# The closing product of batches 3 to 6 split into a second level of seven products, in two parts, with its three adds on GpSimd

## Chip, core and metric

The kernel runs on one core of a Trainium2 chip. The metric is the device time of one execution in microseconds; the median of repeated runs is compared. Engines are named as in the profile: PE is the matrix engine (PEld its weight loads), DVE is VectorE, ACT is ScalarE, POOL is GpSimd, SP issues DMAs.

## What is computed

Inputs are `x` (8 batches, 8 heads, 512 tokens, 64 wide), `state` (8 batches, 8 heads, 32 rows, 64 wide), `w_in` (512 x 2048) and `w_out` (2048 x 512). Cut to what matters:

```python
a  = softmax(x @ state.T / 8);  xread = a  @ state     # 512 rows per batch
a2 = softmax(state @ x.T / 8);  sread = a2 @ x         # 32 rows per batch
rows = concat([xread, sread])                          # 544 rows per batch, 512 wide over the heads
out = gelu(rows @ w_in) @ w_out                        # 4352 x 512
```

## The kernel before

**Batches and slots.** The kernel works through the eight batches. For the batch it is at, `b`, the token rows go through `mm1` (line 506: per block `m` of 128 of the 2048 hidden columns, two matmuls of 512 columns, followed on ACT by the gelu of line 513 into the tile `g`). In the loop over batches 2 to 7 the sixteen blocks are done in eight slots `p`, two blocks each (`M(k, k + 1)`); each slot also does pieces of other work: the second matrix product of the batch before, and the attention of the batch after. The order on each engine is written out by hand: the program order is the queue order of that engine (`manual_schedule`), and semaphores are put where one engine needs another's data or buffer.

**The second product.** `g @ w_out` is not done plainly in batches 1 to 7. The 512 tokens, the 2048 hidden columns and the 512 outputs are each halved, and the eight block products are replaced by seven (named 1 to 7), at the price of sums and differences of blocks. `chain` names the left operand of each; for 5, 6, 7 and 3 it is a sum that DVE makes (`g_sum`, line 637), for 1, 2 and 4 it is a block of `g`. The right operands are blocks of `w_out` or the differences `ws` made once by `w_diff`. One product is `x_mm` (line 647): two blocks of 128 tokens times eight blocks of hidden columns, so 16 matmuls of 256 columns each, with 16 weight loads. The results are combined: `snap` copies a PSUM bank to SBUF on ACT (line 670), `add` on DVE (line 666) makes pieces of the output `oh`.

**Order of the products.** For batch `b`, product 2 is made in slots 5 and 6 and product 4, which this text calls the closing unit, in slot 7 of the batch's own loop (`X(b, "4")`). Products 1, 6, 5 and 7 follow in slots 0 to 3 of the next loop and product 3 in slot 5. The result of product 4 lies in the tile `c4` and is read only in slot 3 of the next loop, by `c21` after product 7. In slot 0 of the next loop the order on PE is: two blocks of `mm1`, then product 1.

**Product 2 is already split once more.** `sub_sums` makes four small sums on DVE (line 721, 128x512 bf16 each). `sub_a` makes four products of four matmuls each, 128 columns wide (line 727), in the four quarters of one PSUM bank, and ACT copies the bank into the tile `qa` (line 741). `sub_b` adds products 6 and 3 to two of the same quarters and overwrites a third with product 7; it therefore has to wait for that copy. ACT copies the bank again into `qb` (line 749), and three DVE adds (line 666, `c<-qb`, `c<-c,qa`, `c<-qa`) put the result `c2` together. Between `sub_a` and `sub_b` stand the two `mm1` blocks of slot 6. `w_subs` (line 595) made the four differences of the weights, `q_w`, early in the kernel.

**Buffers.** The pool `cpool` has one buffer per tag. Before, `qa` uses the tag `s5` and `qb` the tag `u`, which the copies of products 5 and 6 use too. The four PSUM buffers `f` go round among `mm1`, the scores and half of `p_all`; the other four banks (`o0` to `o3`) belong to the products, and slot 5 borrows them for `p_all` (line 441, the product of states and `w_in` for the next batch), whose results ACT and DVE cast into `P` (lines 1002 and 1307). In `p_all` the group `f = 3` writes the bank that product 3 has just used, so it waits for the DVE add `oh<-xp,u` of product 3.

**GpSimd.** In slot 0 POOL waits for a gelu (`hold_for`, line 1016), issues the load of a later batch (`load_x`, line 117) and rearranges the batch after next (`rearr`, line 225), whose transpose SP issues in slot 3 (line 278). In slot 5 it makes the second rearrangement (`rearr_ones`, line 235).

**Last batch.** In the loop of batch 7 `read_out_slot` interleaves the seven products of the 256 state rows (`SR`, line 866) with the products of batch 6.

Of the kernel before, what the change touches and what calls it, by code (L numbers as in the profile page):

```python
# [17 lines left out]
def kernel(  # L18
# [8 lines left out]
    nc = tc.nc  # L27
# [551 lines left out]
        return {"1": b11, "2": b21, "3": b22}.get(name) if name in "123" else w_t[name]  # L579

    QN = NH // 2
    q_w = persist.tile([128, 4, MH // 2, QN], BF16, name="q_w", tag="mix3")

    def w_sub(k, n):
        return b21[:, MH // 2 * k:MH // 2 * k + MH // 2, QN * n:QN * n + QN]

    def w_subs(which):
        for i in which:
            x, y = (
                (w_sub(1, 1), w_sub(1, 0)),  # L590
                (w_sub(0, 1), q_w[:, 0]),
                (w_sub(0, 1), w_sub(1, 1)),
                (w_sub(0, 0), q_w[:, 1]),
            )[i]
            nc.vector.tensor_tensor(out=q_w[:, i], in0=x, in1=y, op=ALU.subtract)

    def sub_rhs(name):
        if name in "123":
            return {"1": w_sub(1, 0), "2": w_sub(0, 0), "3": w_sub(0, 1)}[name]
        return q_w[:, "5674".index(name)]  # L600

    xs = {}
    left, right = slice(0, NH), slice(NH, d_model)
# [68 lines left out]
    def X(b, name):  # L672
        bank = BANK[name]
        first = name in "2154"
        if first:
            xs[b, bank] = otile([128, 2, NH], "xp", bank)
        ps = xs[b, bank]
        x_mm(ps, x_lhs(b, name), w_rhs(name), first)
        if name == "2":
            if b > 1:  # L680
                snap(b, "c2", "c2", ps)
        elif name == "4":
            snap(b, "c4", "c4", ps)
        elif name == "1":
            for h in range(2):
                xs[b, "o", h] = hpool.tile([128, 2, d_model], FP32, name="oh", tag=f"oh{h}")
            add(xs[b, "o", 0][:, :, left], ps, xs[b, "c2"])
            x_out(b, 0, left)
        elif name == "6":
            snap(b, "u", "u", ps)  # L690
        elif name == "5":
            snap(b, "s5", "s5", ps)
# [12 lines left out]
    def c21(b):  # L705
        add(xs[b, "o", 1][:, :, left], xs[b, 1], xs[b, "c4"])

    def sub_q(b):
        def q(h, k):
            g = g_q(b, 0, 0)  # L710
            return g[:, MH // 2 * k:MH // 2 * k + MH // 2, 128 * h:128 * h + 128]

        return q

    def sub_sums(b):
        t = apool.tile([128, 4, MH // 2, 128], BF16, name="gsub", tag="gsum")
        got = xs[b, "sub"] = {}
        for i, name in enumerate("5673"):
            x, y, op = chain(name, sub_q(b), got)
            got[name] = t[:, i]  # L720
            nc.vector.tensor_tensor(out=t[:, i], in0=x, in1=y, op=op)

    def sub_mm(b, name, at, start=False):
        lhs = chain(name, sub_q(b), {})[0] if name in "124" else xs[b, "sub"][name]
        rhs = sub_rhs(name)
        for m in range(MH // 2):
            nc.tensor.matmul(  # L727
                xs[b, 0][:, at, :],
                lhsT=lhs[:, m, :],
                rhs=rhs[:, m, :],  # L730
                start=(start and m == 0),
                stop=(m == MH // 2 - 1),
                skip_group_check=True,
            )

    def sub_a(b):
        xs[b, 0] = otile([128, 4, QN], "xp", 0)
        for at, name in enumerate("2145"):
            sub_mm(b, name, at, at == 0)
        xs[b, "qa"] = cpool.tile([128, 4, QN], FP32, name="qa", tag="s5")  # L740
        nc.scalar.copy(out=xs[b, "qa"], in_=xs[b, 0])

    def sub_b(b):
        sub_mm(b, "6", 1)
        sub_mm(b, "3", 3)
        sub_mm(b, "7", 0, True)
        qa = xs[b, "qa"]
        qb = cpool.tile([128, 4, QN], FP32, name="qb", tag="u")
        nc.scalar.copy(out=qb, in_=xs[b, 0])  # L749
        c = xs[b, "c2"] = c_tile("c2")  # L750
        c = c.rearrange("p j (n w) -> p j n w", n=2)
        add(c[:, 0], qb[:, 1:2, :].broadcast_to([128, 2, QN]), qb[:, 0:4:3, :])
        add(c[:, 1], c[:, 0, 0:1, :].broadcast_to([128, 2, QN]), qa[:, 2:4, :])
        add(c[:, 0, 0, :], qa[:, 1, :], qa[:, 0, :])

    def rows_out(h, js, ns, eng):
        b = B - 1
# [24 lines left out]

    def L5():
        b = B - 1
        xs[b, "s5"] = c_tile("s5")
# [131 lines left out]

    def R(name):
        def c_new(n):
            rs[n] = cpool.tile([128, NH], FP32, name="r_" + n, tag="r_" + n)  # L920
# [19 lines left out]
        snaps = {"2": "c2", "4": "c4", "6": "u", "5": "s5"}  # L940
        if name in snaps:
            nc.scalar.copy(out=c_new(snaps[name]), in_=ps)
        elif name == "1":
            for h in range(2):
                rs["o", h] = opool.tile([128, d_model], FP32, name="osb", tag="osb")
            add(rs["o", 0][:, left], ps, rs["c2"])
        elif name == "7":
            add(rs["o", 1][:, right], ps, rs["s5"])
            add(rs["o", 1][:, left], ps, rs["c4"])
            r_out(1)  # L950
        elif name == "3":
            add(rs["o", 0][:, right], ps, rs["u"])
            r_out(0)
# [73 lines left out]
    def read_out_slot(p):  # L1027
        c, b, k = B - 2, B - 1, 16 * (B - 1) + 2 * p
        if p == 0:
            sr_x("34")  # L1030
            M(k, k + 1)
            g_sum(c, "56")
            SR("3", 0)
            SR("4", 0)
            X(c, "1")
            sr_x("167")
            SR("5", 0)
            SR("2", 0)
            sr_w("7")
        if p == 1:  # L1040
            M(k, k + 1)
            SR_gelu("52", 0)
            X(c, "6")
            SR("1", 0)
            SR("6", 0)
        if p == 2:
            M(k, k + 1)
            SR_gelu("6", 0)
            SR("7", 0)
            SR_gelu("7", 0)  # L1050
            g_sum(c, "7")
            X(c, "5")
            SR("3", 1)
            SR("4", 1)
            g_sum(c, "3")
        if p == 3:
            M(k, k + 1)
            SR("5", 1)
            SR("2", 1)
            SR_gelu("52", 1)  # L1060
            X(c, "7")
            c22(c)
            SR("1", 1)
            c21(c)
            x_out(c, 1)
            SR("6", 1)
        if p == 4:
            M(k, k + 1)
            SR_gelu("6", 1)
            SR("7", 1)  # L1070
            SR_gelu("7", 1)
            X(c, "3")
# [86 lines left out]
    M(8, 9)  # L1159
    M(10, 11)  # L1160
    mm2_m(0, 8)
    w_subs((0, 1))
    atr(1)
    w_subs((2, 3))
    mm2_m(0, 9)
    burst([(1, 1), (0, 3)])
    mm2_m(0, 10)
# [54 lines left out]
    for b in range(2, B):  # L1222
        nb = b + 1
        for p in range(8):
# [24 lines left out]
                w_diff("7")  # L1249
            if p < 5 and nb < B:  # L1250
                if p == 0:
                    g_sum(b - 1, "56")
                if p == 2:
                    if b % 2:
# [23 lines left out]
            if nb == B:  # L1278
                if p == 5:
                    R("2")  # L1280
                    r_sum("73")
                    R("4")
                    sub_sums(b)
                if p == 6:
                    R("1")
                    sub_a(b)
                    R("6")
                    sub_b(b)
                    R("5")
                if p == 7:  # L1290
                    X(b, "4")
# [1 line left out]
            if p == 5:  # L1293
# [11 lines left out]
                sub_a(b)  # L1305
                for _, f, ps in rest:
                    nc.scalar.copy(out=Ps[nb][:, 0, f * 512:(f + 1) * 512], in_=ps[0])
            if p == 6:
                sub_b(b)
# [47 lines left out]
```

## Time and profile before

| what | value |
|---|---|
| median of three runs | 201.92 us (201.89 to 202.7) |
| the profiled execution: its own time | 202.25 us |
| its span in the profile | 200.3 us |
| PE busy | 193.9 us (97%) |
| DVE busy | 155.1 us (77%) |
| ACT busy | 145.6 us (73%) |
| POOL busy | 48.1 us (24%) |
| granted PE clock | 9 tenths or more in every slice; 1.00 in the result |

The profile is of one execution. Its page gives the busy time of each engine, the chain of work that ended last, and groups of instructions with their mean duration. The timeline gives instructions of one engine in order of time, with equal neighbours merged into one row (`x16` is sixteen of them; its second number is from the first start to the last end). Matmuls overlap, so the pace of PE is read from the starts of successive rows, not from the duration of one.

### The profile page before, as it was taken

How to read it: one execution, taken by the hardware profiler on the slowest of the kernel's cores; microseconds unless marked ns; L12 is line 12 of the kernel's file. 1: busy time of each engine (PE TensorE's matmuls, PEld its weight loads, DVE VectorE, ACT ScalarE, POOL GpSimd, SP SyncE). 2: the span in 40 equal slices, each digit the busy share in tenths (PEclk: the TensorE clock that was granted, in tenths of full speed). 3: DMA queues.
4: the chain of work that ended last, by engine and by line, in shares of the span. 5: the costliest groups of instructions: out<-in, count | busy, mean ns of one | idle time of the engine just before them, and what ended most of it. 6: DMA issues, size and time to landing. Idle time of an engine off the chain costs nothing.

```text
span 200.3 us, 5055 instructions
## 1 busy us (share of the span) xinstructions
PE 193.9 (97%) x2102; PEld 134.3 (67%) x2107; DVE 155.1 (77%) x279; ACT 145.6 (73%) x264; POOL 48.1 (24%) x65
## 2 busy tenths in 40 slices
PE   7899999999999999999999999999999999999993
PEld 2533544465767777767777787677776888878893
DVE  2963796969989769975997798849966897984863
ACT  3785577699896799569966997599948778775120
POOL 8972504543403444040504300030000000000000
PEclk9999999999999999999999999999999999999999
DMA  5999999976494959680797025420024010030044
GB/s 192 197 174 202 206 199 201 183 136 142 84 149 77 241 65 164 141 214 0 77 188 209 5 67 95 138 75 27 28 107 106 0 55 0 7 153 0 18 146 157
DMA packets 40567, 23.16 MB, mean 116 GB/s; under 512 B 21856, under 2 KB 39136, under 8 KB 40544
## 3 DMA queue, kind: packets, MB, share of 16 engines
q0 software_dynamic: 13984, 8.10, 29.9%
q1 hardware_dynamic: 25728, 14.22, 27.5%
q10 hardware_dynamic: 832, 0.52, 0.8%
q8 instruction: 16, 0.26, 0.5%
q14 instruction: 7, 0.06, 0.1%
HBM read 17.30 MB, written 8.91 MB: 131 GB/s over the span
## 4 chain that ended last, share of the span: by engine, by line
PE 86%; DMA 5%; POOL 4%; ACT 2%; issue 0%; DVE 0%; POOLq 0%
PE xp L647 36%; PE hp L506 26%; DMA xb<-in_x_dram 5%; PE xp L727 5%; PE op L548 3%; PE sp L866 3%; PE rp L932 3%; POOL w_in_bf L105 2%; PE op L532 2%; PE xp L773 2%; PE pt L333 2%; ACT P L1002 1%; PE p_ps L441 1%; PE sr L962 1%; POOL sbd L95 1%; POOL w_out_bf L113 1%
## 5 line engine op out<-in xcount | busy, mean ns | idle before, releaser
L513 ACT ACTIVATE g<-hp 128x512 bf16<-128x512 f32 x124 | 67.1, 614 | 17.0 <-PE hp L506 16.8
L506 PE MATMUL hp<-AT,P 128*128 128x512 bf16 x248 | 62.2, 379 | 0.0
L647 PEld LDWEIGHTS <-gsum 128*128 128x128 bf16 x416 | 40.4, 98 | 8.9 <-issue 0.4
L647 PE MATMUL xp<-ws,gsum 128*128 128x256 bf16 x320 | 38.2, 273 | 0.0
L506 PEld LDWEIGHTS <-P 128*128 128x128 bf16 x248 | 23.0, 98 | 19.4 <-ACT P L452 0.7
L647 PEld LDWEIGHTS <-g 128*128 128x128 bf16 x240 | 23.3, 98 | 4.8
L637 DVE TENSOR_TENSOR gsum<-g 128x2048 bf16<-128x2048 bf16 x14 | 17.0, 1218 | 0.6 <-ACT g L513 0.6
L225 POOL COPY x<-xb 128x1024 bf16<-128x1024 bf16 x12 | 12.2, 1044 | 18.5 <-DMA xb<-in_x_dram 18.5
L235 POOL COPY xo<-xb 128x1024 bf16<-128x1024 bf16 x12 | 12.2, 1043 | 14.1 <-PE sr L962 13.9
L647 PE MATMUL xp<-w_out_bf,g 128*128 128x256 bf16 x128 | 15.3, 273 | 0.0
L647 PE MATMUL xp<-ws,g 128*128 128x256 bf16 x112 | 13.4, 273 | 0.0
L1016 POOL COPY hold<-g 128x1 bf16<-128x1 bf16 x7 | 2.3, 334 | 42.9 <-ACT g L513 42.9
L666 DVE TENSOR_TENSOR c<-qb 128x256 f32<-128x256 f32 x6 | 2.6, 425 | 12.7 <-ACT qb L749 12.7
L548 PE MATMUL op<-w_out_bf,g 128*128 128x512 bf16 x44 | 11.0, 380 | 0.5 <-issue 0.3
L647 PE MATMUL xp<-w_out_bf,gsum 128*128 128x256 bf16 x96 | 11.5, 273 | 0.0
L666 DVE TENSOR_TENSOR oh<-xp,c 128x512 f32<-128x512 f32 x14 | 9.6, 686 | 2.4 <-PE xp L647 2.0
L1002 DVE CAST P<-p_ps 128x512 bf16<-128x512 f32 x15 | 9.4, 683 | 2.4 <-PE p_ps L441 2.4
L356 DVE TENSOR_TENSOR a<-e,ics 128x512 bf16<-128x512 bf16 x14 | 10.5, 750 | 0.5
L353 DVE TENSOR_REDUCE cs<-e 128x16 f32<-128x512 bf16 x14 | 9.5, 678 | 0.9 <-ACT e L340 0.9
L513 ACT ACT_TABLE_LOAD x7 | 9.0, 1283 | 0.1
L441 PE MATMUL p_ps<-w_in_bf,sbd 64*32 64x512 bf16 x248 | 9.0, 380 | 0.0
L637 DVE TENSOR_TENSOR gsum<-gsum,g 128x2048 bf16<-128x2048 bf16 x7 | 8.6, 1225 | 0.2
(155 smaller groups left out, 308.9 us busy)
## 6 DMA issues: line engine op xcount, KB each, us to landing
out_dram<-oh SPq DMA_DIRECT2D x15, 256.0 KB, 3.3
xb<-in_x_dram POOLq DMA_DIRECT2D x7, 512.0 KB, 7.1
out_dram<-oh SPq DMA_DIRECT2D x6, 512.0 KB, 3.1
w_in_bf<-in_moe_w_in_dram POOLq DMA_DIRECT2D x6, 256.0 KB, 11.7
out_dram<-osb SPq DMA_DIRECT2D x5, 256.0 KB, 3.0
w_out_bf<-in_moe_w_out_dram POOLq DMA_DIRECT2D x4, 256.0 KB, 7.8
w_out_bf<-in_moe_w_out_dram POOLq DMA_DIRECT2D x2, 512.0 KB, 13.3
x0f<-in_x_dram SPq DMA_DIRECT2D x3, 256.0 KB, 3.8
```

Of the source, the lines that this page charges most:

```text
L225: nc.gpsimd.tensor_copy(out=A.x4[:, :, :, 64 * t:64 * t + 64].rearrange("p j c d -> p c j d"), in_=src[:, t],)
L235: eng.tensor_copy(out=A.xo[:, :, :, 2 + 64 * t:66 + 64 * t].rearrange("p j c d -> p c j d"), in_=src[:, t],)
L356: nc.vector.tensor_tensor(out=A.a[:, :, hs].rearrange("p g (c n) -> p g c n", n=NS), in0=e4, in1=ics[:, :, :].to_broadcast((128, G, 2, NS) ...
L441: nc.tensor.matmul(ps[t][32 * c:32 * c + 32, :], lhsT=sbd[64 * t:64 * t + 64, b, c, 32 * t:32 * t + 32], rhs=w_in_bf[64 * t:64 * t + 64, c ...
L506: nc.tensor.matmul(hp, lhsT=Ps[b][:, t, m * 128:(m + 1) * 128], rhs=atts[b].AT[:, :, t, :], start=(t == 0), stop=(t == 1),)
L513: nc.scalar.activation(out=gs[b][:, m, :], in_=hp, func=AF.Gelu)
L548: nc.tensor.matmul(ops[b, j], lhsT=gs[b][:, m, j * 128:(j + 1) * 128], rhs=w_out_bf[:, m, :], start=(m == 0), stop=(m == MC - 1),)
L637: nc.vector.tensor_tensor(out=got[name], in0=x, in1=y, op=op)
L647: nc.tensor.matmul(ps[:, j - js[0], :], lhsT=lhs[:, m, 128 * j:128 * j + 128], rhs=rhs[:, m, :], start=(first and j == js[0] and m == 0), ...
L666: nc.vector.tensor_tensor(out=out, in0=x, in1=y, op=ALU.add)
L727: nc.tensor.matmul(xs[b, 0][:, at, :], lhsT=lhs[:, m, :], rhs=rhs[:, m, :], start=(start and m == 0), stop=(m == MH // 2 - 1), skip_group_ ...
L1002: copy(out=Ps[b][:, t, f * 512:(f + 1) * 512], in_=ps[t])
```

## The change

The closing unit (product 4) of batches 3 to 6 is made like product 2: by `sub_sums`, `sub_a` and `sub_b`, which now take the unit's name. `sub_a(b, "4")` stands where `X(b, "4")` stood, `sub_b(b, "4")` after the two `mm1` blocks of slot 0 of the next loop (for batch 6 in `read_out_slot`). The three adds of unit 4 go to GpSimd. Its weight differences are made by four more DVE subtractions in slot 3 of batch 3. `qa` and `qb` get tags of their own, each shared by both units; the copies of product 5 use the tag of `c2`, and the copies of the last products of the state rows (`R`) use two tiles of the output pool. Batches 1, 2 and 7 keep `X(b, "4")`.

```diff
-    def sub_a(b):
-        xs[b, 0] = otile([128, 4, QN], "xp", 0)
+    def sub_a(b, unit):
+        ps = xs[b, BANK[unit]] = otile([128, 4, QN], "xp", BANK[unit])
         for at, name in enumerate("2145"):
-            sub_mm(b, name, at, at == 0)
-        xs[b, "qa"] = cpool.tile([128, 4, QN], FP32, name="qa", tag="s5")
-        nc.scalar.copy(out=xs[b, "qa"], in_=xs[b, 0])
+            sub_mm(b, unit, name, at, at == 0)
+        xs[b, "qa"] = cpool.tile([128, 4, QN], FP32, name="qa", tag="qa")
+        nc.scalar.copy(out=xs[b, "qa"], in_=ps)
...
-        qb = cpool.tile([128, 4, QN], FP32, name="qb", tag="u")
-        nc.scalar.copy(out=qb, in_=xs[b, 0])
-        c = xs[b, "c2"] = c_tile("c2")
+        qb = cpool.tile([128, 4, QN], FP32, name="qb", tag="qb")
+        nc.scalar.copy(out=qb, in_=xs[b, BANK[unit]])
+        name = "c" + unit
+        c = xs[b, name] = c_tile(name)
...
-        add(c[:, 0], qb[:, 1:2, :].broadcast_to([128, 2, QN]), qb[:, 0:4:3, :])
-        add(c[:, 1], c[:, 0, 0:1, :].broadcast_to([128, 2, QN]), qa[:, 2:4, :])
-        add(c[:, 0, 0, :], qa[:, 1, :], qa[:, 0, :])
+        for out, x, y in (
+            (c[:, 0], qb[:, 1:2, :].broadcast_to(wide), qb[:, 0:4:3, :]),
+            (c[:, 1], c[:, 0, 0:1, :].broadcast_to(wide), qa[:, 2:4, :]),
+            (c[:, 0, 0, :], qa[:, 1, :], qa[:, 0, :]),
+        ):
+            (nc.vector if unit == "2" else nc.gpsimd).tensor_tensor(out=out, in0=x, in1=y, op=ALU.add)
...
                 if p == 0:
+                    if b > 3:
+                        sub_b(b - 1, "4")
                     g_sum(b - 1, "56")
...
                 if p == 3:
-                    sub_sums(b)
+                    sub_sums(b, "2")
+                    if b == 3:
+                        w_subs("4", range(4))
...
-                sub_a(b)
+                sub_a(b, "2")
+                if b > 2:
+                    sub_sums(b, "4")
...
-                X(b, "4")
+                if b > 2:
+                    sub_a(b, "4")
+                else:
+                    X(b, "4")
```

In `read_out_slot`, slot 0, `sub_b(c, "4")` is added after `M(k, k + 1)`, with `c` being batch 6.

More of the change, by code (lines that the diff above doesn't have):

```diff
@@ L581, with w_sub, w_subs, sub_rhs @@
     QN = NH // 2
[L582 to L587, printed above, removed]
+    q_w = {
+        name: persist.tile([128, 4, MH // 2, QN], BF16, name=f"q_w{name}", tag=f"q{name}")
+        for name in "24"
+    }
+    def w_sub(unit, k, n):
+        return w_rhs(unit)[:, MH // 2 * k:MH // 2 * k + MH // 2, QN * n:QN * n + QN]
+    def w_subs(unit, which):
+        t = q_w[unit]
         for i in which:
             x, y = (
[L590 to L593, printed above, removed]
-            )[i]
-            nc.vector.tensor_tensor(out=q_w[:, i], in0=x, in1=y, op=ALU.subtract)
-    def sub_rhs(name):
+                (w_sub(unit, 1, 1), w_sub(unit, 1, 0)),
+                (w_sub(unit, 0, 1), t[:, 0]),
+                (w_sub(unit, 0, 1), w_sub(unit, 1, 1)),
+                (w_sub(unit, 0, 0), t[:, 1]),
+            )[i]
+            nc.vector.tensor_tensor(out=t[:, i], in0=x, in1=y, op=ALU.subtract)
+    def sub_rhs(unit, name):
         if name in "123":
-            return {"1": w_sub(1, 0), "2": w_sub(0, 0), "3": w_sub(0, 1)}[name]
-        return q_w[:, "5674".index(name)]
+            return w_sub(unit, *{"1": (1, 0), "2": (0, 0), "3": (0, 1)}[name])
+        return q_w[unit][:, "5674".index(name)]
     xs = {}
@@ L691, in X @@
         elif name == "5":
-            snap(b, "s5", "s5", ps)
+            snap(b, "s5", "c2", ps)
         elif name == "7":
@@ L706, in c21, with sub_q, sub_sums, sub_mm @@
         add(xs[b, "o", 1][:, :, left], xs[b, 1], xs[b, "c4"])
-    def sub_q(b):
+    def sub_q(b, unit):
+        g = x_lhs(b, unit)
         def q(h, k):
-            g = g_q(b, 0, 0)
             return g[:, MH // 2 * k:MH // 2 * k + MH // 2, 128 * h:128 * h + 128]
         return q
-    def sub_sums(b):
+    def sub_sums(b, unit):
         t = apool.tile([128, 4, MH // 2, 128], BF16, name="gsub", tag="gsum")
-        got = xs[b, "sub"] = {}
+        got = xs[b, "sub", unit] = {}
         for i, name in enumerate("5673"):
-            x, y, op = chain(name, sub_q(b), got)
+            x, y, op = chain(name, sub_q(b, unit), got)
             got[name] = t[:, i]
             nc.vector.tensor_tensor(out=t[:, i], in0=x, in1=y, op=op)
-    def sub_mm(b, name, at, start=False):
-        lhs = chain(name, sub_q(b), {})[0] if name in "124" else xs[b, "sub"][name]
-        rhs = sub_rhs(name)
+    def sub_mm(b, unit, name, at, start=False):
+        raw = name in "124"
+        lhs = chain(name, sub_q(b, unit), {})[0] if raw else xs[b, "sub", unit][name]
+        rhs = sub_rhs(unit, name)
         for m in range(MH // 2):
             nc.tensor.matmul(
-                xs[b, 0][:, at, :],
+                xs[b, BANK[unit]][:, at, :],
                 lhsT=lhs[:, m, :],
@@ L734, in sub_mm, with sub_b @@
             )
-    def sub_a(b):
-        xs[b, 0] = otile([128, 4, QN], "xp", 0)
+    def sub_a(b, unit):
+        ps = xs[b, BANK[unit]] = otile([128, 4, QN], "xp", BANK[unit])
         for at, name in enumerate("2145"):
-            sub_mm(b, name, at, at == 0)
-        xs[b, "qa"] = cpool.tile([128, 4, QN], FP32, name="qa", tag="s5")
[L741 to L746, printed above, removed]
+            sub_mm(b, unit, name, at, at == 0)
+        xs[b, "qa"] = cpool.tile([128, 4, QN], FP32, name="qa", tag="qa")
+        nc.scalar.copy(out=xs[b, "qa"], in_=ps)
+    def sub_b(b, unit):
+        sub_mm(b, unit, "6", 1)
+        sub_mm(b, unit, "3", 3)
+        sub_mm(b, unit, "7", 0, True)
         qa = xs[b, "qa"]
-        qb = cpool.tile([128, 4, QN], FP32, name="qb", tag="u")
-        nc.scalar.copy(out=qb, in_=xs[b, 0])
-        c = xs[b, "c2"] = c_tile("c2")
+        qb = cpool.tile([128, 4, QN], FP32, name="qb", tag="qb")
+        nc.scalar.copy(out=qb, in_=xs[b, BANK[unit]])
+        name = "c" + unit
+        c = xs[b, name] = c_tile(name)
         c = c.rearrange("p j (n w) -> p j n w", n=2)
-        add(c[:, 0], qb[:, 1:2, :].broadcast_to([128, 2, QN]), qb[:, 0:4:3, :])
-        add(c[:, 1], c[:, 0, 0:1, :].broadcast_to([128, 2, QN]), qa[:, 2:4, :])
-        add(c[:, 0, 0, :], qa[:, 1, :], qa[:, 0, :])
+        wide = [128, 2, QN]
+        for out, x, y in (
[4 more added lines that the diff above has]
+            (nc.vector if unit == "2" else nc.gpsimd).tensor_tensor(out=out, in0=x, in1=y, op=ALU.add)
     def rows_out(h, js, ns, eng):
@@ L784, in L5 @@
         b = B - 1
-        xs[b, "s5"] = c_tile("s5")
+        xs[b, "s5"] = c_tile("c2")
         for ps, j, n0, n1 in l_mm("5", True):
@@ L919, in c_new @@
         def c_new(n):
-            rs[n] = cpool.tile([128, NH], FP32, name="r_" + n, tag="r_" + n)
+            if "homes2" not in rs:
+                rs["homes2"] = [
+                    t[:, NH * i:NH * i + NH]
+                    for t in [opool.tile([128, d_model], FP32, name="rt", tag="osb") for _ in range(2)]
+                    for i in range(2)
+                ]
+            rs[n] = rs["homes2"].pop()
             return rs[n]
@@ L1031, in read_out_slot @@
             M(k, k + 1)
+            sub_b(c, "4")
             g_sum(c, "56")
@@ L1161 @@
     mm2_m(0, 8)
-    w_subs((0, 1))
+    w_subs("2", (0, 1))
     atr(1)
-    w_subs((2, 3))
+    w_subs("2", (2, 3))
     mm2_m(0, 9)
@@ L1282 @@
                     R("4")
-                    sub_sums(b)
+                    sub_sums(b, "2")
                 if p == 6:
                     R("1")
-                    sub_a(b)
+                    sub_a(b, "2")
                     R("6")
-                    sub_b(b)
+                    sub_b(b, "2")
                     R("5")
@@ L1304 @@
                     rearr_ones(nb + 1)
-                sub_a(b)
+                sub_a(b, "2")
+                if b > 2:
+                    sub_sums(b, "4")
                 for _, f, ps in rest:
@@ L1308 @@
             if p == 6:
-                sub_b(b)
+                sub_b(b, "2")
             if p == 7:
```

## The prediction

> **What bounds the kernel now.** I read the page first: the busy lines, then the chain that ended last, then the groups.
>
> ```profile
> PE 193.9 (97%) x2102; PEld 134.3 (67%) x2107; DVE 155.1 (77%) x279; ACT 145.6 (73%) x264; POOL 48.1 (24%) x65
> ...
> PE 86%; DMA 5%; POOL 4%; ACT 2%; issue 0%; DVE 0%; POOLq 0%
> ```
>
> The chain is PE nearly throughout, so any time taken from PE's queue is won and any wait put into it is lost, unless PE would have stopped later anyway. The timeline from 67 to 177 us has one stop of PE per batch, in slot 5, where the copy of the first `p_all` bank must end before `sub_a` (the chain of waits shows 0.38 + 0.51 us of ACT there in batch 4). ACT itself has idled just before that for 1.47 to 1.80 us, waiting for PE, so this stop moves along with PE and absorbs nothing.
>
> Next the timeline around both units of batch 4, all engines together.
>
> ```profile
> 109.52 0.61 PE L727 MATMUL xp<-w_out_bf,g 128*128 128x128 bf16 x8
> ...
> 110.41 1.03 PE L506 MATMUL hp<-AT,P 128*128 128x512 bf16 x4
> 110.61 0.58 ACT L741 COPY qa<-xp 128x512 f32<-128x512 f32 x1 [0.16 <-PE xp L727]
> ...
> 111.27 0.39 PE L727 MATMUL xp<-q_w,gsub 128*128 128x128 bf16 x4
> ...
> 111.94 1.03 PE L506 MATMUL hp<-AT,P 128*128 128x512 bf16 x4
> 112.04 1.12 ACT L513 ACTIVATE g<-hp 128x512 bf16<-128x512 f32 x2
> ...
> 112.80 1.91 PE L647 MATMUL xp<-ws,g 128*128 128x256 bf16 x16
> 113.01 0.63 ACT L749 COPY qb<-xp 128x512 f32<-128x512 f32 x1
> 113.47 1.16 ACT L513 ACTIVATE g<-hp 128x512 bf16<-128x512 f32 x2
> 113.67 0.42 DVE L666 TENSOR_TENSOR c<-qb 128x256 f32<-128x256 f32 x1 [1.00 <-ACT qb L749]
> 114.13 0.42 DVE L666 TENSOR_TENSOR c<-c,qa 128x256 f32<-128x256 f32 x1
> 114.55 1.03 PE L506 MATMUL hp<-AT,P 128*128 128x512 bf16 x4
> 114.59 0.29 DVE L666 TENSOR_TENSOR c<-qa 128x128 f32<-128x128 f32 x1
> 114.75 0.58 ACT L670 COPY c<-xp 128x512 f32<-128x512 f32 x1
> 115.24 1.08 ACT L513 ACTIVATE g<-hp 128x512 bf16<-128x512 f32 x2
> 115.41 1.91 PE L647 MATMUL xp<-w_out_bf,g 128*128 128x256 bf16 x16
> ```
>
> Two things are to be seen. PE starts one row when the one before has been issued, without a gap. ACT has no gap from 111.09 to 114.63 either: it is behind PE here, and in unit 2 its copy of `qa` ends at 111.19, only 0.08 us before `sub_b` at 111.27 needs it.
>
> **Closing unit, PE alone.** Product 4 takes 114.55 - 112.80 = 1.75 us for 16 matmuls (109 ns each). In small products, by unit 2: part one 110.41 - 109.52 = 0.89, part two 111.94 - 111.27 = 0.67, together 1.56 us for 28 matmuls (55.6 ns each, weight loads of 98 ns hidden). That is -0.19 us a batch, -0.76 us in four.
>
> These rows oppose a rule. The Trainium skill, "TensorE: Matmul & The Clock Gate", section "Back-to-back issue gap", puts a stream of load-and-multiply pairs with 128 columns at about 81 ns. By it 28 would take 2.27 us, an estimate, and the unit would lose 0.5 us instead of winning 0.19. The rows of unit 2 are the same operation here, and they decide.
>
> **The wait that comes with it.** `sub_b` of unit 4 cannot start before ACT has copied its bank into `qa`. The new order on PE is part one from 112.80 to 113.69, the two `mm1` blocks to 114.55, then `sub_b`. The copy needs three things: the matmuls done (113.69 + 0.17 of drain = 113.86); ACT free, which has the gelus of slot 7 ahead of it until 114.63; and the buffer `qa` free. Unit 4 uses the same single buffer as unit 2, and the last DVE add of unit 2 reads it until 114.59 + 0.29 = 114.88. That is the latest. With 0.04 us to ACT, 0.585 for the copy (its row outside overlaps) and 0.05 to PE, `sub_b` starts at 115.56, so PE waits 1.01 us. Net for the batch: 1.01 - 0.19 = **+0.82 us**. The same sum in batches 3 and 5, whose last adds end at 93.60 and 135.73 and whose blocks would end at 93.27 and 135.40, also gives 1.01. In batch 6 the add ends at 156.97 and PE is free at 156.75: a wait of 0.90. There the next product (line 866, state rows) waited for DVE until 157.69; it would now start at 157.65 + 0.67 = 158.32, **+0.63**.
>
> Queued behind that copy on ACT are the gelus of slot 0, the new copy of `qb`, the load of the exp table and the scores. PE needs none of them before the blocks of slots 2 and 3, and ACT, which had 0.46 to 0.57 us idle before the copy of product 5 in slot 2 and 1.47 in slot 4, catches up there. So I count the wait once a batch and no more.
>
> **New weight differences.** Four DVE subtractions of the size of `q_w` (0.42 us, starts 0.34 to 0.45 apart) stand in slot 3 of batch 3 ahead of the add `oh<-xp,u`.
>
> ```profile
> 86.03 0.42 DVE L721 TENSOR_TENSOR gsub<-g,gsub 128x512 bf16<-128x512 bf16 x1
> 86.68 0.69 DVE L666 TENSOR_TENSOR oh<-xp,u 128x512 f32<-128x512 f32 x1 [0.24 <-PE xp L647]
> ...
> 87.00 1.16 PE L441 MATMUL p_ps<-w_in_bf,sbd 64*32 64x512 bf16 x32
> ```
>
> They would start at 86.37 and the add at 87.85 instead of 86.68; it ends at 88.54. The last eight of the 32 matmuls of `p_all` write the bank that it reads. They stood at about 87.60 and cannot start before 88.58. Eight at 25 ns end at 88.8, and `sub_a` of unit 2 starts there instead of at 88.23: **+0.6 us**, once. Bounds: 0.35 if the starts are 0.34 apart and the drain is hidden, 0.85 if each takes its full 0.42 and the pipeline refills.
>
> **Other DVE work.** `sub_sums` of unit 4 is four times 0.42, 1.55 us by starts. In batches 3 and 5 DVE idles 2.78 us before the adds of unit 2, in batch 6 1.86 us: hidden. In batch 4 it idles 1.00 us, but one `srm` just before took 1.15 us instead of 0.29 beside two POOL copies (110.11 to 112.13), which the change moves later; 1.00 + 0.86 = 1.86 covers it. Without that the adds, the `qa` copy and the wait grow by 0.55 us in this batch.
>
> **GpSimd.** The trace has no two-input add on POOL. From below a copy of one element (0.19 us), from above the copy of 1024 elements (1.04 us), so 0.6 to 3.1 for three; I take 1.4, between them by size. They start at about 116.7 and `c4` is read by `c21` some 9 us later (126.43 in the trace): no cost on the path at either end. Behind them on POOL are `hold_for`, the load and `rearr`, so in batch 4 `rearr` ends about 3 us later and SP issues the transpose later (98.12 before). Its result is read a batch later, and SP's next issue is at 105.96, so nothing waits. POOL beside DVE has a price: besides `srm`, one `a<-e,ics` took 1.51 us instead of 0.69 and a pair `srw` 2.57 instead of 1.28 while POOL copied. DVE has 0.43 us in hand before product 7 in slot 3 of batch 4, and PE's own delay adds 0.8. I count zero, with up to 0.8 in all as upper end; below zero nothing, since POOL's moved copies free DVE only where PE does not wait for it.
>
> The Trainium skill, "GPSIMD Engine Reference", section "Key points", says the shared SBUF interfaces contend with DVE instructions that have two SBUF inputs. That would let the adds slow DVE's sums `gsum`, as an estimate by less than the 0.8 above; no row of before has this pair.
>
> **Moved at no cost.** The copies of `R` into output tiles and product 5's into `c2`: earlier readers finish over 2 us before. The third PSUM copy per batch (0.63 us of ACT) is in the chain above.
>
> **Sum.** 3 x 0.82 + 0.63 + 0.6 = +3.7 us. The profiled execution would go from 202.25 to 205.95, its span from 200.3 to 204.0. The median shown is 0.33 below that execution: **205.6 us**.
>
> **Rivals.**
> 1. *The wait is only ACT's queue.* If the buffer `qa` comes free earlier than worked out, the copy ends at 115.11 and PE waits 0.62, 0.50 in batch 6: 3 x 0.43 + 0.23 = 1.5 us, with 0.35 to 0.6 for the differences 1.9 to 2.1, so about **203.9**. For it: ACT's backlog is certain. Against it: the add that frees the buffer ends later in all four batches.
> 2. *More waits.* DVE is slowed beside POOL (0.8), the adds of batch 4 are late (0.55) and the differences cost 0.85: 3.7 + 1.6, so **207.2**. Against it: the slack above.
> 3. *Not slower.* The copy of `qa` ends before the two blocks of slot 0 do, and only -0.76 is left: **201.1**. The place is the first matmul of `sub_b`, the price 0.9 to 1.0 a batch, and the turning point is the last add of unit 2 ending 1.0 us earlier (113.87 in batch 4) and ACT's gelus of slot 7 done by then too. For it: unit 2 just manages the same, by 0.08. Against it: in unit 2 ACT was idle before its copy, and here it is not.
>
> **Chances.** Forecast 0.68, rival 1 0.14, rival 2 0.10, rival 3 0.08. The range 203.4 to 207.2 holds the first three with their bounds (its low end is rival 1 with the smallest terms and a smaller wait by 0.1 in each batch). A measurement can tell about 0.5% from no change. Rival 3 lies within that (-0.4%); a third of it goes to faster: faster 0.03, same 0.06, slower 0.91.
>
> **What would show it.** Right: in slot 0 of batches 4 to 7 PE idle about 1 us before its first line-733 matmul, released by the ACT copy `qa`, which itself was released by a DVE add; `p_all` of batch 3 stretched by about 0.6. Part one and two of unit 4 at 0.89 and 0.67. Wrong if PE idles 0.6 or not at all there, if DVE or POOL is what PE waits for in slots 1 to 3, or if the small matmuls are not at 55.6 ns.

## The result, and the profile after

| what | before | after |
|---|---|---|
| median | 201.90 us (201.85 to 202.70; the three runs and a fourth) | 207.59 us (207.22 to 208.07, 4 runs) |
| the profiled execution: its own time / its span | 202.25 / 200.3 us | 207.22 / 205.4 us |
| first matmul of the first product of batch 1 (`x_mm`: line 647 before, 651 after), by the chain view, to the start of the last DVE add | 42.61 to 197.32 = 154.71 us | 42.59 to 201.44 = 158.85 us |
| start of that add to the end of the span | 2.98 us | 3.96 us |

The ratio is 1.0274, 95% interval [1.0254, 1.0295]: slower. The forecast was 205.6 us with a range up to 207.2; direction and place were right, but the measured time lies above the range: the size was too small by 2.0 us. The last two rows already say where: 4.14 us more in the body of the kernel, for which the prediction had 3.7, and 0.98 us more at its end, for which it had nothing. (The body is counted from the first product of batch 1, as that product's start moves by about 1.5 us among the profiled executions of this document. Spans are printed to a tenth, so the ends are good to 0.05 us.)

The page of after, busy line and chain; a percentage in the chain is a share of the span by the engine that carried it.

```profile
PE 194.1 (94%) x2155; PEld 134.0 (65%) x2155; DVE 163.3 (80%) x299; ACT 147.8 (72%) x268; POOL 58.2 (28%) x77
...
PE 78%; ACT 5%; DMA 5%; DVE 5%; POOL 4%; issue 1%; ACTq 0%; POOLq 0%; DVEq 0%
```

PE is busy as long as before (194.1 us against 193.9) in a span 5.1 us longer, and the chain has moved off it: PE 78% where it was 86%, DVE 5% where it was 0%, ACT 5% where it was 2%. So PE's work has not grown; waits were put between its instructions. The waits view of after names them (total us, count, the longest):

```profile
PE xp L733 <- ACT qa L747: 3.6, 4, 0.9
...
PE p_ps L441 <- DVE oh L670: 0.7, 1, 0.7
```

And who holds that copy up, in the same view:

```profile
ACT qa L747 <- DVE c L765: 1.4, 4, 0.4
```

Neither PE wait was there before. The timeline of after around the closing unit of batch 4, the same place as the prediction's rows of before, without the rows of weight loads:

```profile
114.38 0.61 PE L733 MATMUL xp<-ws,g 128*128 128x128 bf16 x8
...
114.83 0.39 PE L733 MATMUL xp<-q_w,g 128*128 128x128 bf16 x4
115.05 0.39 PE L733 MATMUL xp<-q_w,gsub 128*128 128x128 bf16 x4
115.08 1.15 ACT L513 ACTIVATE g<-hp 128x512 bf16<-128x512 f32 x2
115.27 1.03 PE L506 MATMUL hp<-AT,P 128*128 128x512 bf16 x4
...
115.74 0.42 DVE L765 TENSOR_TENSOR c<-c,qa 128x256 f32<-128x256 f32 x1
116.20 0.29 DVE L765 TENSOR_TENSOR c<-qa 128x128 f32<-128x128 f32 x1
...
116.60 0.59 ACT L747 COPY qa<-xp 128x512 f32<-128x512 f32 x1 [0.36 <-DVE c L765]
...
117.23 0.38 PE L733 MATMUL xp<-q_w,gsub 128*128 128x128 bf16 x4 [0.94 <-ACT qa L747]
...
117.90 1.91 PE L651 MATMUL xp<-w_out_bf,g 128*128 128x256 bf16 x16
...
118.82 0.73 POOL L765 TENSOR_TENSOR c<-qb 128x256 f32<-128x256 f32 x1 [7.19 <-ACT qb L755]
119.63 0.73 POOL L765 TENSOR_TENSOR c<-c,qa 128x256 f32<-128x256 f32 x1
```

This is the chain of the prediction, link by link. The two `mm1` blocks start at 115.27 and would be through 0.86 later, at 116.13. ACT has ended its gelus at 116.23 and then idles 0.36 us, because the buffer `qa` is still read by the last add of unit 2, which ends at 116.49. The copy starts 0.11 later, PE goes on at 117.23. From the first matmul of unit 4 to the first of product 1 it was 2.61 us before (112.80 to 115.41) and is 3.52 now (114.38 to 117.90).

The other wait, at `p_all` of batch 3:

```profile
86.83 0.84 PE L441 MATMUL p_ps<-w_in_bf,sbd 64*32 64x512 bf16 x24
...
87.33 0.42 DVE L599 TENSOR_TENSOR q_w<-ws,q_w 128x512 bf16<-128x512 bf16 x1
...
87.66 0.68 DVE L670 TENSOR_TENSOR oh<-xp,u 128x512 f32<-128x512 f32 x1
...
88.40 0.41 PE L441 MATMUL p_ps<-w_in_bf,sbd 64*32 64x512 bf16 x8 [0.72 <-DVE oh L670]
...
88.74 0.62 PE L733 MATMUL xp<-w_out_bf,g 128*128 128x128 bf16 x8
```

The add `oh<-xp,u` starts behind the last of the four weight differences, and the last eight matmuls of `p_all` wait for it. From the first of the 32 to `sub_a` it is 1.91 us (86.83 to 88.74), where it was 1.23 before (87.00 to 88.23): 0.68 more.

The end of the program. Two views of the transfers: first before, then after, the issues of the last two small outputs (engine's queue, count, KB each, median us from issue to landing).

```profile
out_dram<-oh SPq DMA_DIRECT2D x1, 64.0 KB, 2.0
out_dram<-oh ACTq DMA_DIRECT2D x1, 64.0 KB, 1.7
```

```profile
out_dram<-oh SPq DMA_DIRECT2D x1, 64.0 KB, 3.1
out_dram<-oh ACTq DMA_DIRECT2D x1, 64.0 KB, 2.8
```

The queues in one stretch of after, 201.4 to 202.4 us, in which these outputs are written (packets, MB, share of 16 engines):

```profile
q1 hardware_dynamic: 248, 0.24, 70.3%
q10 hardware_dynamic: 125, 0.12, 34.1%
q14 instruction: 1, 0.01, 7.5%
```

The same two transfers land 1.1 us later. What lies among them in after, and not in before, is one packet on the queue `q14 instruction`, a block of program being fetched (8 such packets on the page, 7 before). The experiments below ask whether that is the cause.

### The profile page after: what moved, and what is told of

It reads as the page before. It is cut to its first block, busy times and chain, and to the rows that moved or that the text cites. A ratio compares the mean times of both kernels' runs of the same rounds, so it can differ in the third digit from the quotient of the medians.

```text
span 205.4 us, 5204 instructions
## 1 busy us (share of the span) xinstructions
PE 194.1 (94%) x2155; PEld 134.0 (65%) x2155; DVE 163.3 (80%) x299; ACT 147.8 (72%) x268; POOL 58.2 (28%) x77
## 4 chain that ended last, share of the span: by engine, by line
PE 78%; ACT 5%; DMA 5%; DVE 5%; POOL 4%; issue 1%; ACTq 0%; POOLq 0%; DVEq 0%
PE xp L651 31%; PE hp L506 22%; PE xp L733 7%; DMA xb<-in_x_dram 5%; PE op L548 4%; PE sp L877 3%; PE rp L949 3%; DVE c L765 2%; POOL w_in_bf L105 2%; PE op L532 2%; PE xp L784 2%; PE pt L333 2%; ACT g L513 2%; PE p_ps L441 1%; ACT qa L747 1%; PE sr L979 1%
## 5 line engine op out<-in xcount | busy, mean ns | idle before, releaser
L670 DVE TENSOR_TENSOR oh<-xp,c 128x512 f32<-128x512 f32 (+1 forms) x22 | 14.2, 663 | 6.7 <-PE xp L651 5.1
L651 PEld LDWEIGHTS <-g 128*128 128x128 bf16 x176 | 16.9, 98 | 2.7
L733 PE MATMUL xp<-q_w,gsub 128*128 128x128 bf16 x120 | 11.6, 219 | 3.6 <-ACT qa L747 3.6
L765 POOL TENSOR_TENSOR c<-qb 128x256 f32<-128x256 f32 x4 | 3.7, 923 | 39.8 <-ACT qb L755 39.8
L733 PEld LDWEIGHTS <-gsub 128*128 128x128 bf16 x160 | 10.2, 97 | 6.6 <-issue 5.3
L356 DVE TENSOR_TENSOR a<-e,ics 128x512 bf16<-128x512 bf16 x14 | 12.6, 900 | 0.5
L548 PE MATMUL op<-w_out_bf,g 128*128 128x512 bf16 x48 | 11.8, 380 | 0.0
L1033 POOL COPY hold<-g 128x1 bf16<-128x1 bf16 x7 | 2.8, 404 | 28.7 <-ACT g L513 28.7
L674 ACT COPY c<-xp 128x512 f32<-128x512 f32 x10 | 6.0, 596 | 4.8 <-PE xp L651 4.6
```

The lines of the kernel that those rows point to most:

```text
L356: nc.vector.tensor_tensor(out=A.a[:, :, hs].rearrange("p g (c n) -> p g c n", n=NS), in0=e4, in1=ics[:, :, :].to_broadcast((128, G, 2, NS) ...
L548: nc.tensor.matmul(ops[b, j], lhsT=gs[b][:, m, j * 128:(j + 1) * 128], rhs=w_out_bf[:, m, :], start=(m == 0), stop=(m == MC - 1),)
L651: nc.tensor.matmul(ps[:, j - js[0], :], lhsT=lhs[:, m, 128 * j:128 * j + 128], rhs=rhs[:, m, :], start=(first and j == js[0] and m == 0), ...
L670: nc.vector.tensor_tensor(out=out, in0=x, in1=y, op=ALU.add)
L733: nc.tensor.matmul(xs[b, BANK[unit]][:, at, :], lhsT=lhs[:, m, :], rhs=rhs[:, m, :], start=(start and m == 0), stop=(m == MH // 2 - 1), sk ...
```

## The experiments

**Theory** after the result: four terms. (a) the wait for `qa`, about 0.9 net in each of batches 3 to 5 and somewhat less in batch 6; (b) 0.6 to 0.7 for the weight differences; (c) about 1 us at the end of the program, from a program fetch among the last outputs; (d) nothing from GpSimd's adds. **Rival**: the waits are symptoms, and VectorE's added work (155.1 to 163.3 us busy) is what the change costs. Times are medians; each ratio is to runs of before that were made beside it. "Body" and "end" are the last two rows of the first table.

### 1. The two predicted waits, one at a time

Weight differences made in slot 5 of batch 2, where VectorE has time (`e1_weights_early`):

```diff
                 if p == 3:
                     sub_sums(b, "2")
-                    if b == 3:
-                        w_subs("4", range(4))
...
                 if b > 2:
                     sub_sums(b, "4")
+                else:
+                    w_subs("4", range(4))
```

> One part moved: the four weight subtractions of unit 4 stand in slot 5 of batch 2, in VectorE's idle stretch of 1.9 us, instead of ahead of an add that PE waits for in batch 3. Theory (the new time is four waits for the qa buffer, one stall from these subtractions, and about 1 us at the end of the program): PE's stop in p_all of batch 3 (0.72 us in the trace) goes, so 207.6 - 0.7 = 206.9 us. Rival (the stop is only the first of several and PE would stop at the next waiter anyway): 207.3 to 207.6 us.

Measured 207.13 us (206.88 to 207.73), ratio 1.0257 [1.0226, 1.0287]. The wait of `p_ps` for `oh` is gone, and the body is 158.20, 0.65 less than after. The end is as in after (3.98). (b) is confirmed by the trace; the medians alone (-0.46) would not carry it.

Part two of unit 4 moved behind the blocks of slot 1, or for batch 6 of slot 1 in the last loop, so that nobody needs `qa` so soon (`e2_part_two_later`):

```diff
                 if p == 0:
-                    if b > 3:
-                        sub_b(b - 1, "4")
                     g_sum(b - 1, "56")
...
+                if p == 1 and b > 3:
+                    sub_b(b - 1, "4")
                 if p < 4:
                     X(b - 1, "1657"[p])
```

> One part moved: part two of unit 4 (its last twelve matmuls, the copy qb and the three GpSimd adds) stands one slot later, ahead of product 6 instead of product 1, so that the copy qa has more than 3 us. Theory: the four waits of 0.94 us for that copy go, 207.6 - 3.8 = 203.8 us, and 0.76 of what is left is the smaller product already counted. Rival (ScalarE and VectorE are too full for the extra copy and sums, and PE stops elsewhere): the chain shows new stops in slots 1 to 3, 205.5 us or more.

Measured 204.95 us (204.56 to 205.41), ratio 1.0145 [1.0115, 1.0175]. The waits of line 733 for `qa` are gone and the body falls by 1.44 to 157.41, not by the 3.6 that they held: other stops stand in their place. The time lies between the theory's 203.8 and the rival's 205.5, with 0.83 of the gain from a shorter end (3.13, see part 4). The next kernel shows them without (b).

Both moves together (`e3_both_moves`):

> Both moves of the two runs beside it. Theory: 207.6 - 0.7 - 3.8 = 203.1 us; against the kernel before that is the win of 0.76 us on PE and a loss of 1 us or more at the end of the program, where the trace shows output DMAs landing later. Rival (no loss at the end, it was chance of one profile): 201.9 - 0.8 = 201.1 us.

Measured 203.85 us (203.68 to 204.48), ratio 1.0096 [1.0065, 1.0126]; body 156.65, end 3.02. The expected 203.1 was missed by 0.75, although the loss at the end that it counted in did not come. The waits view:

```profile
PEld L651 <- DVE gsum L641: 1.8, 1, 1.8
PEld L877 <- DVE srx L855: 1.3, 1, 1.3
PE xp L651 <- DVE gsum L641: 1.3, 1, 1.3
...
PE sp L877 <- ACT qa L747: 0.8, 1, 0.8
```

The body is still 1.94 above before, although the small unit saves 0.76. By the starts of its rows, set against those of before, PE loses 1.4 us before product 7 in batch 4 (the stop of 1.27), 0.9 before the state rows in the last loop, where `srx` now is late (the weight loads stand 1.3 us there and the matmuls 0.8), and about 0.25 for a gelu in batch 5: 2.55 - 0.76 = 1.8, and the rest is in smaller pieces. The first of these stops in the timeline of this kernel:

```profile
96.22 3.52 DVE L837 TENSOR_TENSOR srw<-w_in_bf 128x1024 bf16<-128x1024 bf16 x2
...
96.56 2.02 POOL L225 COPY x<-xb 128x1024 bf16<-128x1024 bf16 x2
...
101.09 1.05 POOL L765 TENSOR_TENSOR c<-c,qa 128x256 f32<-128x256 f32 x1
101.47 1.75 DVE L641 TENSOR_TENSOR gsum<-g 128x2048 bf16<-128x2048 bf16 x1
...
102.22 1.32 POOL L765 TENSOR_TENSOR c<-qa 128x128 f32<-128x128 f32 x1
...
103.28 1.92 PE L651 MATMUL xp<-ws,gsum 128*128 128x256 bf16 x16 [1.27 <-DVE gsum L641]
```

The pair `srw` takes 3.52 us beside two POOL copies (1.28 undisturbed, 2.57 before), the sum `gsum` 1.75 beside an add of unit 4 (1.22 undisturbed), and that engine's next add 1.32 instead of 0.46. PE, no longer held for `qa`, asks for this sum earlier than in after, and it is late. With the two waits gone, VectorE beside GpSimd is what is late next. So something like the rival holds for what is left, not for what after lost.

### 2. Buffer or queue: what holds the copy?

Unit 4 gets a buffer for `qa` that unit 2 does not read (`e4_qa_not_shared`):

```diff
-        xs[b, "qa"] = cpool.tile([128, 4, QN], FP32, name="qa", tag="qa")
+        xs[b, "qa"] = cpool.tile([128, 4, QN], FP32, name="qa", tag="qa" if unit == "2" else "u")
```

> One part undone: the copy qa of unit 4 goes to the buffer that product 6 uses later (tag u), so it no longer waits for the adds of unit 2 to read theirs. Nothing else moves. Theory (the shared buffer decides, and ScalarE's queue is what is next late): the copy starts when the gelus of slot 7 end, about 0.45 us earlier, so PE waits 0.5 instead of 0.94 a batch: 207.6 - 1.8 = 205.8 us. Rival (ScalarE's queue was the limit all along): 207.6 us. Rival (the wait was the buffer alone): 203.8 us.

Measured 205.85 us (205.41 to 206.92), ratio 1.0199 [1.0152, 1.0245]; body 157.71, end 3.02.

```profile
PE xp L733 <- ACT qa L747: 1.7, 4, 0.5
...
PE xp L651 <- DVE gsum L641: 0.5, 1, 0.5
```

The wait falls from 0.94 to 0.47 in batch 3, and ACT no longer idles before the copy: it comes straight behind a gelu, at 94.51 in this trace, while the add of unit 2 reads its own buffer until 94.96. So the buffer was the last of the three conditions and ACT's queue the next, as the prediction ordered them. So the expected 205.8 was met in part by luck: of the 1.9 us that left these waits 1.14 are won in the body; part of the rest came back as the stop of 0.5 before product 7. The end, which nobody had counted in, is 0.94 shorter too (part 4). (The first product is 0.8 us later in this execution, which is why the time fell by less than these two together.)

### 3. Is VectorE's own time the point?

The three adds of unit 4 on VectorE, in the same place of the program (`e8_adds_on_vector`: `nc.vector` for both units).

> One part undone: the three adds of unit 4 on VectorE instead of GpSimd. Theory (GpSimd's adds cost nothing on the path, and nothing is won by them that VectorE could not give): VectorE gets 1.3 us more ahead of the sums of slot 0, whose results product 6 needs. They ended about 2 us before it in the trace after, so 207.6 to 208.2 us. Rival (GpSimd beside VectorE is what costs): faster by 0.5 us or more. Rival (VectorE is full): slower by 2 us or more.

Measured 219.79 us (218.96 to 220.62), ratio 1.0875 [1.0839, 1.0911]: far beyond what was expected. The timeline of this kernel at the start of the loop of batch 4:

```profile
95.67 0.59 ACT L755 COPY qb<-xp 128x512 f32<-128x512 f32 x1
...
96.29 2.74 DVE L765 TENSOR_TENSOR c<-qb 128x256 f32<-128x256 f32 x1 [2.29 <-ACT qb L755]
96.71 2.02 POOL L225 COPY x<-xb 128x1024 bf16<-128x1024 bf16 x2
...
99.72 1.22 DVE L641 TENSOR_TENSOR gsum<-g 128x2048 bf16<-128x2048 bf16 x1
101.05 1.23 DVE L641 TENSOR_TENSOR gsum<-gsum,g 128x2048 bf16<-128x2048 bf16 x1
102.19 0.68 DVE L670 TENSOR_TENSOR oh<-xp,c 128x512 f32<-128x512 f32 x1
...
102.92 2.59 PE L651 MATMUL xp<-ws,gsum 128*128 128x256 bf16 x16 [4.27 <-DVE oh L670]
```

The adds cost 1.1 us of VectorE a batch, the kernel 3 us a batch. The first add stands in VectorE's queue ahead of the sums for products 5 and 6; VectorE idles 2.29 us for ACT's copy `qb`, the add then takes 2.74 us beside POOL, and the sums start at 99.72 where in after they started at 94.09. The add `oh` behind them is what PE waits for, 4.27 us. So GpSimd relieved first of all a place in VectorE's queue; VectorE's busy time in this run is 167.4 us, 77% of the span.

Part of the 12 us is the clock of PE. From 103.98 to 107.39, right after this stop, the profile shows a granted clock of 0.50, and product 7 takes 2.59 us there instead of 1.91. Half of these 3.4 us, 1.7 as an estimate, is lost in addition to the stop.

The same adds on VectorE, but late, in slot 3 just before `c21` reads them, on top of both moves (`e11_late_adds_on_vector`). This was to free POOL and VectorE from each other and remove the 1.27 us of `e3_both_moves`:

```diff
+        if unit == "2":
+            sub_adds(b, unit, qa, qb)
+        else:
+            xs[b, "late"] = (qa, qb)
...
     def c21(b):
+        if (b, "late") in xs:
+            sub_adds(b, "4", *xs[b, "late"])
```

> Both moves of e3, and the three adds of unit 4 on VectorE, put directly ahead of the add that reads them in slot 3. Theory (what is left in e3 is VectorE slowed beside GpSimd's adds: a sum of 1.75 us instead of 1.22 and PE's stop of 1.27 us before product 7 in batch 4): that stop halves, and 1.15 us of VectorE in slot 3 is covered, 203.85 - 0.7 = 203.2 us. Rival (VectorE's time is short, whoever makes the adds): 203.9 to 205 us, with PE stopped in p_all by the add of product 3.

Measured 208.61 us (208.43 to 209.33), ratio 1.0341 [1.0322, 1.0360]: missed. The stop before product 7 did shrink, from 1.27 to 0.53. But VectorE's next sums now meet POOL's second rearrangement:

```profile
109.29 2.29 POOL L235 COPY xo<-xb 128x1024 bf16<-128x1024 bf16 x2 [9.68 <-PE sr L987]
109.41 1.26 DVE L728 TENSOR_TENSOR gsub<-g 128x512 bf16<-128x512 bf16 x1
...
110.59 1.25 DVE L728 TENSOR_TENSOR gsub<-g,gsub 128x512 bf16<-128x512 bf16 x1
...
111.77 0.68 DVE L670 TENSOR_TENSOR oh<-xp,u 128x512 f32<-128x512 f32 x1
...
112.50 0.43 PE L441 MATMUL p_ps<-w_in_bf,sbd 64*32 64x512 bf16 x8 [2.11 <-DVE oh L670]
```

The adds push the sums `gsub` under POOL's copies, where each takes 1.25 us instead of 0.42; `oh<-xp,u` is late and `p_all` stands 2.11 us. It is term (b) again, three times as large. Behind this stop, too, the granted clock is 0.50 for 3.4 us (112.76 to 116.17), and `p_all` of batch 5 stands another 0.50. The body is 160.16 and the end 3.96.

### 4. The end of the program

The first theory was that more instructions on VectorE and PE move their program fetches into the last outputs. Before with 20 more tiny VectorE instructions at its start (`e5_before_pad_vector`), with 98 more PE instructions (`e6_before_pad_pe`, the warming matmuls at the start cut into smaller ones, 49 more with 49 weight loads), and with both (`e7_before_pad_both`):

```diff
-    nc.vector.memset(spare, 0.0)
+    for _ in range(21):
+        nc.vector.memset(spare, 0.0)
...
-    keep_warm(28)
+    keep_warm(28, 0.5)
```

> The kernel before, with 20 more writes of a one-element constant on VectorE in its idle start, so that VectorE's program is as long as after the change (275 instructions). Theory (the loss of 1 us at the end comes from fetching one more block of VectorE's program while the last outputs are written): the span ends about 3.9 us after the start of the last add instead of 3.0, 201.9 + 1 = 202.9 us. Rival (the longer program has nothing to do with it): 201.9 us.

> The kernel before, with the first dummy matmuls for the clock cut into 56 of 64 columns instead of 7 of 512, so that PE's program has 98 more instructions (after the change 96 more). Theory (the loss at the end comes from fetching one more block of PE's program, which the trace after shows at 200.4 us of 205.4): 202.9 us. Rival (it comes from VectorE's block, or from neither): 201.9 us.

> The kernel before with both paddings. Theory (program blocks fetched during the last outputs): 202.9 us, the fetches of both queues in the last 4 us, and the last output landing about 1 us later. Rival: 201.9 us, and the loss at the end of the changed kernel is something else.

Measured 202.14, 202.09 and 202.24 us, ratios 1.0008 [0.9984, 1.0033], 0.9994 [0.9970, 1.0018] and 1.0008 [0.9994, 1.0022]; ends 2.94, 3.05 and 3.07 us. No effect. This theory fell for both engines: their longer programs bring no packet of `q14` into the last 5 us, and the other instruction queue, `q8`, whose last packet comes 4.1 us before the end in `e6` and `e7`, changes nothing there. What is left in the counts is ScalarE: the trace holds 312 instructions of every kind on it before and 324 after. So before with 12 more tiny ScalarE copies (`e9_before_pad_scalar`), and after with 16 more, which should bring the fetch ahead of the outputs (`e10_after_pad_scalar`):

```diff
     X(b, "1")
+    for i in range(0, 6):
+        nc.scalar.copy(out=pads[:, i:i + 1], in_=spare)
     g_sum(b, "7")
```

> The kernel before, with twelve one-element copies on ScalarE in its two idle stretches of 2.9 and 3.9 us before the last copies. Theory (the 1 us at the end of the changed kernel is the fetch of one more block of ScalarE's program, which has 324 recorded instructions there, 312 before; with 323 the fetch came 1.5 us before the end, with 326 4.5 us, with 324 in the midst of the last outputs): such a fetch appears in the last 5 us and the last output lands up to 1 us later, 202.2 to 203.1 us. Rival (it follows VectorE's or GpSimd's length): no such fetch, 202.1 us.

> The changed kernel, with sixteen one-element copies on ScalarE in the same two idle stretches. Theory (as for the run beside it): the fetch moves ahead of the last outputs, the span ends about 3.0 us after the start of the last add instead of 4.0, 207.6 - 1.0 = 206.6 us. Rival (the end of the changed kernel is long for another reason): 207.6 us.

`e9_before_pad_scalar`: 202.97 us (202.53 to 203.09) against 201.88, ratio 1.0051 [1.0036, 1.0066], end 3.81 us. The queues of this kernel from 198.3 to 199.3 us, three to two us before the end of its span:

```profile
q10 hardware_dynamic: 232, 0.14, 47.6%
q1 hardware_dynamic: 144, 0.07, 23.9%
q14 instruction: 1, 0.01, 4.3%
```

Twelve copies of one element cost 1.09 us, three quarters of it behind the last computing instruction (3.81 - 2.98), with a fetch among the outputs as in after. The likeness is not complete: here only the last output of ACT's queue lands later (2.6 us instead of 1.7; SP's 2.0 as before), in after both. `e10_after_pad_scalar`: 206.91 us (205.83 to 208.80), ratio 1.0260 [1.0200, 1.0319]; its profiled execution has the body of after (158.86) and an end of 3.36. That agrees, but the runs scatter by 3 us and it would not decide alone. All traces with another number of ScalarE instructions, by that number:

| kernels | ScalarE instructions | the fetch before the end of the span | end |
|---|---|---|---|
| before | 312 | none in the last 4 us | 2.98 us |
| `e12` (below) | 321 | none in the last 4 us | 3.09 us |
| `e2`, `e3`, `e4` | 323 | 1 to 2 us | 3.13, 3.02, 3.02 us |
| after, `e1`, `e9`, `e11` | 324, 324, 324, 325 | 2 to 4 us | 3.96, 3.98, 3.81, 3.96 us |
| `e8` | 326 | over 4 us | 3.37 us |
| `e10` | 340 | earlier | 3.36 us |

With 323 instructions the fetch falls at the end of the last outputs or behind them, with 324 or 325 among them, and only these four ends are about a microsecond longer. That the fetch delays the outputs fits all rows; shown is that ScalarE's instructions alone bring both. By which way (the same DMA engines, or the queues before them), and why the end of `e8` and `e10` is 0.4 longer with an earlier fetch, no run here tells.

The Trainium skill, "Runtime: NRT & Kernel Launch", section "Instruction fetch mechanics", has the sequencer stream its program in blocks by DMA and calls the price of crossing into a new block mostly hidden. In the middle of this kernel the other fetches cost nothing that the trace shows; in the last 4 us the measurement differs, with 0.8 to 1.0 us.

### 5. What is left without batch 6

Both moves, and the small unit in batches 3 to 5 only (`e12_not_in_batch_6`): `2 < b < 6` in place of `b > 2` for `sub_a` and `sub_sums`, and no `sub_b` in the last loop.

> Both moves of e3, with batch 6 left as it was before the change (product 4 in one piece). Theory (in batch 6 the smaller unit wins nothing, since the next product on PE waits for VectorE's srx, 1.3 us in e3): 203.85 + 0.2 at most if the wait is only covered by the longer unit, and 203.2 if the extra sums, copy and adds of unit 4 also delay srx there. Rival (the stop is unrelated to unit 4): 204.0 us or more.

Measured 203.35 us (202.84 to 203.53), ratio 1.0069 [1.0052, 1.0087]. The wait of the weight loads for `srx` falls from 1.3 to 0.4, as before the change, and the body by 0.65 to 156.00, so the second figure of the theory (203.2) is the one that holds. The stop before product 7 in batch 4 remains:

```profile
PE xp L651 <- DVE gsum L641: 1.3, 1, 1.3
```

This is the fastest version that was run with the change in it, and it is still slower than before.

## Why the prediction was wrong, and what of it held

The sum failed at a step that it does not have. It carries the profiled execution from 202.25 to 205.95 us by stops of PE alone, and so puts the time behind the last computing instruction at nothing, without a reason. The runs showed 0.98 us more there; without it the median would have been about 206.6, inside the range. (Without the scatter of the median, 0.7 us below, it would have been inside too, but that is no step of the mechanism.) The wait and the weight differences, the mechanism that the sum does have, came as described.

Each of its steps, in us, in the profiled execution:

| step | predicted | measured | from |
|---|---|---|---|
| the small unit by itself, a batch | -0.19 | -0.19 | 0.89 (114.38 to 115.27) and 0.67 (117.23 to 117.90) |
| wait and small unit, batches 3, 4, 5 | +0.82 each | +0.91 each | 2.61 before, 3.52 after, in all three |
| the same, batch 6 | +0.63 | +0.72 | 2.69 before (155.00 to 157.69), 3.41 after (158.50 to 161.91) |
| weight differences | +0.6 | +0.68 | 1.23 before, 1.91 after, at `p_all` of batch 3 (a stop of 0.72); `e1_weights_early` gives 0.65 back |
| GpSimd's adds, VectorE beside them, and the rest of the body | 0 | +0.01 | what remains: 4.14 - 0.68 - 2.73 - 0.72; in it PE reaches `p_all` of batch 3 0.15 earlier, and part two of unit 2 starts 0.04 to 0.05 later in each of four batches |
| end of the program | not in the sum | +0.98 | 2.98 and 3.96 |
| start, and what lies around the span | 0 | -0.15 | 42.61 and 42.59; 1.95 and 1.82 |
| sum | +3.7 | +4.97 | 202.25 and 207.22 |

**What held.** The closing unit: 28 small matmuls at 55.6 ns, no slower in the new place. The wait, not the matmuls, is what the change cost. The wait: its place, the engine that releases it and the DVE add that releases that engine are those named, and `e4_qa_not_shared` shows the order of the conditions, so rival 1 (only ACT's queue) is refused for after and right for a kernel with another buffer. The weight differences: to 0.08. GpSimd's adds at no cost on the path: 0.73 + 0.73 + 0.46, about 1.9 where 1.4 was taken (one first add took 1.51), ready at about 98.6 and read some 8 us later. That ACT catches up and PE waits only once a batch held in after.

**Mis-sized: the wait.** 0.09 a batch too small, 0.36 in all. The step "with 0.04 us to ACT" is the one: 0.11 were measured (94.18 to 94.29, 116.49 to 116.60), and the last add ended another 0.03 later against PE.

**Missing: the end of the program.** This is the step that failed. The prediction let what lies behind the last computing instruction stay as it was, and did not name it. It counted the instructions that the change adds on VectorE and GpSimd for their time; that ScalarE's few extra ones also move its next program fetch, and that it would land among the last outputs, was no step of it. With +0.98 it is the largest single error. `e5` to `e7` refuse the explanation by VectorE or PE, `e9_before_pad_scalar` reproduces most of it (0.83) in before by ScalarE alone.

**Chosen wrongly: the median.** The prediction subtracted 0.33 because the execution profiled before stood that far above its median. After's stood 0.37 below. These 0.7 us are scatter between executions of one kernel; the other executions have no trace, and what differed in them stays open. So 2.0 us of error are 0.98 + 0.36 + 0.7, with the small remainders against each other.

**Rival 2** reached the range's upper end, 207.2, by stops that did not come: VectorE slowed beside POOL on the path, and the late adds of batch 4. In after the timeline shows no stop of PE for them: PE comes late enough to the products, having stood for `qa`. `e3_both_moves` and `e11_late_adds_on_vector` lay them open, with 1.27 and 2.11 us.

## What to carry to other kernels

When a product is split so that its second part needs a PSUM copy, the price is the chain from its last reader of the buffer to the copy to PE; write out every condition of the copy with its time, and after removing the last, expect the next one at once, as here buffer, then ACT's queue, then VectorE's sums. An add that waits for another engine costs what stands behind it in its queue: the same three adds cost nothing on GpSimd, where they take 1.9 us a batch, and about 12 us in four batches on VectorE, where they take 1.1. And look at the last microseconds by themselves: a handful of tiny instructions on one engine can move a program fetch among the last outputs, so a difference of 1 us in a short kernel need not come from the change's work.

## What was not expected of the hardware

**VectorE and GpSimd block each other for whole instructions.** In `e3_both_moves` the first of the two `srw` starts at 96.22 and ends only 0.56 us after POOL's two copies (96.56 to 98.58); in `e8_adds_on_vector` an add of 0.42 us takes 2.74 and ends 0.30 after them (99.03, 98.73); in `e11_late_adds_on_vector` sums of 0.42 take 1.25, one POOL copy each. It works the other way too: POOL's add of 0.46 takes 1.32 while the sum of line 641 runs. These DVE instructions all have two inputs in SBUF. The Trainium skill, "SBUF — State Buffer", section "SBUF: two separate sides", describes an exclusive lock on a shared port pair, held for a whole instruction, and not a share of the bandwidth; the durations in these rows agree. One thing in them stays open: the `srw` and the add of `e8` start 0.3 to 0.4 us ahead of POOL's first copy and still end only behind the second. The prediction had priced it as a slowdown of up to 0.8 in all; as a block its price is what is left of the other engine's instructions.

**A program fetch among the last outputs** goes with an end that is 0.8 to 1.0 us longer (the table in part 4).

**After a long stop PE's granted clock is halved for a while.** In `e8_adds_on_vector` (a stop of 4.27 us) and `e11_late_adds_on_vector` (2.11 us) the granted clock is 0.50 for 3.4 us, from 1.1 and 0.3 us after the end of the stop. Behind the shorter stops of these traces (between the first product of batch 1 and the last add), up to 1.96 us in `e8`, it stays at 1.00. A stop of that length thus costs about 1.7 us more than itself, an estimate from half of the 3.4.
